# Turned weights of an attention training step: one TensorE pass that stores them, in place of crossbar loads in each stage

## The chip, the cores and the metric

One NeuronCore of a Trainium2 chip runs the whole program. The metric is device time in microseconds (us) of one execution. Three timed runs of the kernel before gave 5001.88, 5009.69 and 5017.44 us; the median is 5009.69 us.

## What is computed

The reference runs a layer and its backward pass. A layer norm gives `xn`. A recurrent attention with 32 heads of 128 walks over 64 segments of 32 tokens; 8 memory rows come out of each segment's output and go into the next. A gated MLP works on the same `xn`.

```python
for s in range(n_seg):                       # 64 segments, one after the other
    h = concat([mem, xn[32*s : 32*s+32]])    # 8 + 32 rows of 640
    q, k, v = h @ Wq, h @ Wk, h @ Wv         # 640 -> 32 heads x 128
    o = softmax(mask(q @ k.T * scale)) @ v @ Wo
    mem = o[:8]; outs.append(o[8:])
s = concat(outs)
g = silu((silu(xn @ w1) * (xn @ w3)) @ w2)
out = x + s * g                              # and the gradients of all nine inputs
```

The forward pass multiplies by Wq, Wk, Wv and Wo. The backward pass multiplies by their transposes. Each of the four weights is 640 x 4096 numbers of bf16, which is 5.24 MB.

## The kernel before

The program is a row of stages; in each stage a call of `in_order` pins the order on every engine to the order in which the code is written.

- **Layer norm and MLP forward** (`phase12_ln_Bfwd`). It also loads Wv and Wk, and ends with projecting the first 672 tokens on Wv.
- **First projections** (`first_part`). The 672 tokens are projected on Wk and then on Wq: 48 steps, each of two banks of five matmuls (L366), a copy of each bank on VectorE and ScalarE, and a 224 KB store on GpSimd's queue (L371). The staging tile `b0st` has three buffers. Six crossbar loads bring the turned tokens `b0x` (L270). Wq and Wo are loaded in nine pieces on ScalarE's queue (L435) in the even steps. The memory rows mem0 are loaded turned, element by element, on GpSimd's queue (L412) at the start of the stage. kT, which the recurrence uses, is cleared by GpSimd memsets (L438). From step 26 on, eight loads `kr` on SyncE's queue (L420) are turned by TensorE (L426).
- **Recurrence** (`recurrence`), 64 dependent segments with the work of all other rows filled into the gaps.
- **Output stage** (`phase3b_out`). 32 units are walked in order: load attention rows `orow` on SyncE's queue (L852), turn them on TensorE (L862), multiply by Wo (L873). From unit 7 on, blocks of `grad_out @ Wo^T` (`gox`, L818) are filled in, which read WoT. The three turned weights WoT, WvT and WkT come in by twelve crossbar loads of 1.31 MB each (`turned_load`, L270), one each in the first four units and then one in every third.
- **Backward recurrence** (`phase4_Abwd`). A prologue of 21 iterations, with 19 units of work for rows, fills in all that the first backward segments need: unit loads on GpSimd's queue (gqv L1169 and L265, gPr L1173), stores of VTD (L1186), DSR (L1217) and GX (L821) on the same queue, stores of GXP (L1233) and loads of gor (L265) on SyncE's queue. Sixteen `gox` blocks ride along; they need the crossbar load `gx` of token rows (SyncE) before block 0 and block 8, and they share one staging tile `gstg`. Four crossbar loads bring WqT, in iterations 1, 4, 7 and 10. Then 64 segments run backward; `packed_half` (L306) reads WoT, `packed_out` (L325) reads WvT, WkT and WqT, all from SBUF.
- **Weight gradients** (`phase6_Awgrads`), eight rounds of four heads. Each round loads three turned weight pieces of 0.66 MB (`ld_w`, L1368) by crossbar into single buffers. In the first round these stand on SyncE's queue between the loads of units 0 to 2 and of units 3 and 4; in the later rounds they are issued before the round's 64 us of `wg` matmuls (L1476).
- **Wo gradient, MLP backward**, which the change doesn't touch.

Of the kernel before, what the change touches and what calls it, by code (L numbers as in the profile page):

```python
# [9 lines left out]
BF16 = mybir.dt.bfloat16  # L10
# [6 lines left out]
P = 128  # L17
# [23 lines left out]
class K:  # L41
# [109 lines left out]
    def setup_dram(self):  # L151
# [45 lines left out]
            self.VTD.append(mk(f"VTD{tl}", (P, ns, H, 40)))  # L197
        self.PM = mk("PM", (T, P, 80))
        self.GSP = mk("GSP", (8, 3, 160, 512))

    def x_src(self, tl, w, c0, c1):
        return self.tok_src(96 * tl, self.geo(tl)[2], w, c0, c1)
# [95 lines left out]
    return ap  # L298


def packed_half(k, bank, x, W, b):

    for dc in range(k.DC):
        for g in range(4):
            c0 = g * 1024 + b * 512
            k.nc.tensor.matmul(bank[32 * g:32 * g + 32, :], x[:, dc, :], W[:, dc, c0:c0 + 512],  # L306
                               start=(dc == 0), stop=(dc == k.DC - 1), tile_position=(0, 32 * g),
                               skip_group_check=True)

# [44 lines left out]
    return pt  # L354


def first_rows(k, ps, stage, xs, off, W, dst, x0, cg, nb=112, tag="b0pb", w=1024, q=None):

    nc = k.nc
    for b in range(2):  # L360
        c0 = cg * 1024 + b * 512
        if w == 512 or b == 0:
            st = stage()
        pb = ps.tile([nb, 512], F32, name="b0pb", tag=tag)
        for dc in range(k.DC):
            nc.tensor.matmul(pb[:], xs[:, dc, x0 - off:x0 - off + nb], W[:, dc, c0:c0 + 512],  # L366
                             start=(dc == 0), stop=(dc == k.DC - 1))
        s0 = b * 512 if w == 1024 else 0
        k.copy(st[:, s0:s0 + 512], pb[:], eng='vs'[b])
        if w == 512 or b == 1:  # L370
            (q or nc.sync).dma_start(dst[x0:x0 + nb, cg * 1024 + (b * 512 if w == 512 else 0):cg * 1024 + b * 512 + 512], st[:])  # L371
# [21 lines left out]
def first_part(k, Wv, Wk_, Wq, Wo, kTs, vt, hxs, rest):  # L393
    nc, tc = k.nc, k.tc
    DC, H, HD = k.DC, k.H, k.HD
    with tc.tile_pool(name="b0", bufs=1) as io, tc.tile_pool(name="b0s", bufs=3) as stp, \
            tc.tile_pool(name="b0p", bufs=4, space=bass.MemoryType.PSUM) as ps, \
            tc.tile_pool(name="b0k", bufs=2, space=bass.MemoryType.PSUM) as pk:
        start = len(nc.cur_bb.bb.instructions)
        xs = io.tile([P, DC, k.NB0], BF16, name="b0x")  # L400
        for x0 in range(0, k.NB0, 112):
# [3 lines left out]
        fetch = [(Wq[:, dc], wq[:, dc]) for dc in range(DC)] + [(Wo[:, h:h + 8], wo[:, h:h + 8]) for h in range(0, H, 8)]  # L405
        for tt in hxs:
            nc.gpsimd.memset(tt[:], 0.0)
        zero = [kTs[0]] + [vt, kTs[1]] + rest
        nc.gpsimd.dma_start(k.m_rows(k.HRO, 0), k.mem0)
        with nc.allow_non_contiguous_dma(reason="tiny mem0 transpose load"):  # L410
            for dc in range(DC):
                nc.gpsimd.dma_start(hxs[0][:, dc, 0:8], k.mem0[:, dc * P:(dc + 1) * P].rearrange("m p -> p m"))  # L412
        rt = io.tile([P, DC, 96], BF16, name="ride0")
        turned_load(k, rt[:], k.XN[k.NB0:k.NB0 + 96, :])
        nc.gpsimd.tensor_copy(hxs[0][:, :, 8:32], rt[:, :, 0:96:4])
# [2 lines left out]
        def kload(i):  # L418
            krs[i] = io.tile([96, 512], BF16, name="kr0", tag="kr0", bufs=2)
            nc.sync.dma_start(krs[i][:], k.KX[0:96, 512 * i:512 * i + 512])  # L420

        def kturn(i):
# [4 lines left out]
            dst = kTs[0][:, i * 4:i * 4 + 4, :].rearrange("p h (s c) -> p h s c", c=40)[:, :, :, 8:40]  # L427
            nc.vector.tensor_copy(dst, pt[:].rearrange("p h (s c) -> p h s c", c=32))

        n = 0  # L430
        for W, dst in ((Wk_, k.KX[:, :]), (Wq, k.QVX[:, 0])):
            for x0 in range(0, k.NB0, 112):
                for cg in range(4):
                    if n % 2 == 0 and fetch:
                        nc.scalar.dma_start(*fetch.pop(0))  # L435
                    first_rows(k, ps, lambda: stp.tile([112, 1024], BF16, name="b0st", tag="b0st"), xs, 0, W, dst, x0, cg, q=nc.gpsimd)
                    if zero:
                        nc.gpsimd.memset(zero.pop(0)[:], 0.0)  # L438
                    if n >= 26 and n % 2 == 0 and (n - 26) // 2 < 9:
                        i = (n - 26) // 2  # L440
                        if i > 0:
                            kturn(i - 1)
                        if i < 8:
                            kload(i)
                    if n == 44:
                        for i in range(2):
                            nc.sync.dma_start(vt[64 * i + 8:64 * i + 40, :], k.QVX[0:32, 1, 2048 * i:2048 * i + 2048])
                    n += 1
# [364 lines left out]
def gx_block(k, xs, sg, pb, WoT, x0, cg, b, eng):  # L813

    w = min(P, k.S - x0)
    c0 = cg * 1024 + b * 512
    for dc in range(k.DC):
        k.nc.tensor.matmul(pb[0:w, :], xs[:, dc, 0:w], WoT[:, dc, c0:c0 + 512], start=(dc == 0), stop=(dc == k.DC - 1))  # L818
    k.copy(sg[0:w, b * 512:(b + 1) * 512], pb[0:w, :], eng='vs'[b])
    if b == 1:  # L820
        eng.dma_start(k.GX0[x0 - k.GB0:x0 - k.GB0 + w, cg * 1024:(cg + 1) * 1024], sg[0:w, :])  # L821


def phase3b_out(k, Wo, W0, W4):
# [2 lines left out]
    nc, tc = k.nc, k.tc  # L827
    D, DC, H, HD, T = k.D, k.DC, k.H, k.HD, k.T
    WT = {}
    WoT = W0.tile([P, DC, HD], BF16, name="WoT", tag="w0")  # L830
    src = k.A_Wo.rearrange("h e d -> (h e) d")
    fetch = [(WoT[:, :, r:r + 1024], src[r:r + 1024, :]) for r in range(0, HD, 1024)]
    for (nm_, src, tag) in (("v", k.A_Wv, "w1"), ("k", k.A_Wk, "w2")):
        WT[nm_] = (W0 if tag == "w1" else W4).tile([P, H, D], BF16, name=f"W{nm_}T", tag=tag)
        src = src.rearrange("d h e -> d (h e)")
        fetch += [(WT[nm_][:, h0:h0 + 8, :], src[:, h0 * P:(h0 + 8) * P]) for h0 in range(0, H, 8)]
    with tc.tile_pool(name="oio", bufs=1) as io, tc.tile_pool(name="oac", bufs=1, space=bass.MemoryType.PSUM) as pa, \
            tc.tile_pool(name="ops", bufs=3, space=bass.MemoryType.PSUM) as ps:
        NRT = k.NO // 4
# [76 lines left out]
        for i, (b, qd) in enumerate(work):  # L916
            if i + 4 < len(work):
                ld(*work[i + 4])
            if fetch and (len(fetch) > 8 or i % 3 == 0):
                turned_load(k, *fetch.pop(0))  # L920
            if i + 1 < len(work):
                turn(*work[i + 1])
            proj(b, qd)
            if late:
                rows_out(*late.pop(0))
            if qd == 7:
                ep_a(b)
                late = [(b, t) for t in range(blocks[b][1])]
            for _ in range(1 if b < 2 else 3):
                if i >= 7 and g0:  # L930
                    gox(*g0.pop(0))
# [8 lines left out]
    n = k.NTL - 1  # L940
# [19 lines left out]
def phase4_Abwd(k, out2, WoT, WvT, WkT, WqT, later):  # L960
# [3 lines left out]
    with tc.tile_pool(name="gst", bufs=1) as st, tc.tile_pool(name="gchain", bufs=1) as ch, \  # L964
# [339 lines left out]
        for i in range(len(pro) + 2):  # L1304
# [2 lines left out]
                    f(*pro[i - o])  # L1307
            if 0 <= i - 2 and (i - 2 + 6 < len(pro) or i >= len(pro) - 2):
                ld_next()
            if i % 3 == 1 and i < 12:  # L1310
                h0 = 8 * (i // 3)
                turned_load(k, WqT[:, h0:h0 + 8, :], k.A_Wq.rearrange("d h e -> d (h e)")[:, h0 * P:(h0 + 8) * P])
            if g0 and i > 0:
                gox(*g0.pop(0))
        assert not g0
# [13 lines left out]
def phase6_Awgrads(k, X, out0, out3, out4, out5):  # L1329
# [12 lines left out]
    with tc.tile_pool(name="h6i", bufs=3) as io, tc.tile_pool(name="h6", bufs=1) as hp, \  # L1342
# [18 lines left out]
            return f"a{base + i % m}"  # L1361

        def ld_w(qd):
            c0 = qd * 512
            ws = []
            for i, src in enumerate((k.A_Wv, k.A_Wk, k.A_Wq)):
                w = gp.tile([P, 4, D], BF16, name="w6", tag=f"w6{i}")
                turned_load(k, w[:], src.rearrange("d h e -> d (h e)")[:, c0:c0 + 512])  # L1368
                ws.append(w)
            Ws[qd] = ws  # L1370

# [723 lines left out]
```

## Time and profile before

| stage | from, us | to, us |
|---|---|---|
| layer norm, MLP forward, first Wv projection | 0 | 282.5 |
| first projections | 282.5 | 412.9 |
| recurrence | 412.9 | 1757 |
| output stage | 1757 | 1882 |
| backward recurrence, prologue | 1882 | 2021 |
| backward recurrence, 64 segments | 2021 | 3132 |
| weight gradients, eight rounds | 3132 | 4420 |
| Wo gradient, MLP backward | 4420 | 4991 |

The profiled execution took 4992.93 us itself; its recorded span is 4991.2 us, so 1.7 us lie around it. It is 16.8 us faster than the median of the three timed runs. Over the span TensorE is busy for 4497.8 us (90%), VectorE for 2211.8 us, ScalarE for 1680.4 us, GpSimd for 1969.0 us; the 16 DMA engines move 836.04 MB, 168 GB/s on average. TensorE's mean granted clock is 0.961.

How to read it: a line of the windows view gives a stretch of time, its length, and then for each engine the time that it was busy and how many instructions it ran, then the granted TensorE clock, the mean busy share of the DMA engines, and the GB/s that they moved. A busy share of DMA can pass 1 in the records. In the view of one source line, "a/b/c" is the shortest, median and longest duration in ns; `SPq` is SyncE's queue, whose durations are times in which the queue issues a transfer, not the transfer itself.

### The profile page before, as it was taken

Reading aid. Unit: us, or ns where it says so; the run is one execution under the profiler, and the core shown is the slowest. Engines: PE = TensorE matmul, PEld = TensorE weight load, DVE = VectorE, ACT = ScalarE, POOL = GpSimd, SP = SyncE. Lnnn points to the kernel's source line nnn. Section 1 sums busy time; section 2 is a strip of 40 time slices with the busy share of each in tenths; the row PEclk is TensorE's granted clock in tenths of the full one; section 3 lists DMA queues with packets and bytes.
Section 4 is the critical chain, followed back from the end, with each engine's and each line's share of the span. In section 5 each row is a group of like instructions: output and inputs, shape, how many; then the busy total and the mean of one; then the engine's idle time right before and its main releaser. Section 6 shows DMA issues by size and latency. Waiting matters only on the chain.

```text
span 4991.2 us, 160105 instructions
## 1 busy us (share of the span) xinstructions
PE 4497.8 (90%) x64274; PEld 2891.4 (58%) x64544; DVE 2211.8 (44%) x7173; ACT 1680.4 (34%) x4768; POOL 1969.0 (39%) x3320
## 2 busy tenths in 40 slices
PE   8888998988898784789999999799999999999999
PEld 4445555555555552556666665556666566667675
DVE  8624555555556522445555554322333233311361
ACT  5422555555555521233333332322233222300000
POOL 6521444444444404345544443533444333411340
PEclk9999999999999886899999999899999999999999
DMA  8653555555555488677777775843565445659783
GB/s 275 219 178 111 164 168 165 168 166 169 165 163 160 127 194 163 175 202 216 214 210 207 205 205 147 179 113 108 130 146 130 107 109 132 164 169 226 163 192 94
DMA packets 1041986, 836.04 MB, mean 168 GB/s; under 512 B 594859, under 2 KB 927391, under 8 KB 1039239
## 3 DMA queue, kind: packets, MB, share of 16 engines
q1 hardware_dynamic: 817639, 547.28, 41.4%
q0 software_dynamic: 127664, 229.32, 16.5%
q10 hardware_dynamic: 95939, 49.18, 3.9%
q8 instruction: 510, 8.36, 0.7%
q14 instruction: 234, 1.91, 0.1%
HBM read 463.32 MB, written 306.24 MB: 154 GB/s over the span
## 4 chain that ended last, share of the span: by engine, by line
PE 48%; DMA 8%; issue 4%; DVE 2%; ACT 2%; SPq 1%; POOL 1%; ACTq 0%; POOLq 0%; DVEq 0%
PE wg L1476 10%; PE gbank L325 8%; PE g L1457 7%; PE oa L1618 3%; DMA dS<-DSR 3%; PE wa L2005 2%; PE pgxb L1938 2%; PE r6p L1408 2%; PE t6g L1439 1%; PE gbank L1086 1%; PE gbank L306 1%; SPq L270 1%; PE pghb L1917 1%; PE sT L873 1%; PE w2a L1861 1%
## 5 line engine op out<-in xcount | busy, mean ns | idle before, releaser
L1476 PE MATMUL wg<-gr,hr 128*128 128x512 bf16 x2352 | 519.1, 379 | 2.5
L1457 PE MATMUL g<-w,ghacc 128*128 128x320 bf16 x3072 | 472.2, 305 | 0.8
L1476 PEld LDWEIGHTS <-hr 128*128 128x128 bf16 x2400 | 233.9, 98 | 278.9
L1457 PEld LDWEIGHTS <-ghacc 128*128 128x128 bf16 x3072 | 294.0, 100 | 110.5 <-ACT ghacc L92 2.2
L713 POOL DMA_DIRECT2D OR<-xv x163 | 93.1, 571 | 452.2 <-ACT xv L712 337.2
L306 PEld LDWEIGHTS <-hx 128*32 128x32 bf16 x7680 | 177.2, 96 | 162.5 <-issue 1.0
L90 DVE CAST wgo<-wg 128x512 bf16<-128x512 f32 x72 | 49.8, 692 | 471.2 <-PE wg L1476 462.9
L90 DVE CAST stg<-bank 128x512 bf16<-128x512 f32 x256 | 177.1, 692 | 179.8 <-PE bank L306 176.0
L92 ACT COPY ghacc<-t6g 128x768 bf16<-128x768 bf16 (+1 forms) x176 | 137.2, 780 | 350.9 <-PE t6g L1439 348.1
L664 ACT ACTIVATE xP<-xsp,xnm 120x120 bf16<-120x120 f32 (+1 forms) x704 | 240.6, 376 | 9.3 <-DVE xnm L660 5.6
L325 PEld LDWEIGHTS <-gkv 128*8 128x8 bf16 x8192 | 178.8, 87 | 83.5 <-issue 3.4
L1186 POOL DMA_DIRECT2D VTD<-gvT x176 | 129.2, 740 | 237.5 <-ACT gvT L1185 209.4
L1423 POOL DMA_DIRECT2D GSP<-grs x48 | 25.7, 547 | 476.9 <-ACT grs L1415 475.2
L675 POOL TENSOR_TENSOR xP<-xP,xrz 120x480 bf16<-120x480 bf16 x163 | 161.7, 992 | 125.2 <-ACT xP L664 88.7
L1463 DVE TENSOR_TENSOR ghacc<-ghacc,g 128x320 f32<-128x320 f32 x192 | 93.6, 487 | 223.3 <-PE g L1457 223.3
L92 ACT CAST wgo<-wg 128x512 bf16<-128x512 f32 x48 | 28.1, 586 | 479.8 <-PE wg L1476 421.4
L1215 DVE SCALAR_TENSOR_TENSOR gdS<-gdp,Dx,gPr 120x120 bf16<-120x120 f32 (+1 forms) x680 | 183.0, 332 | 0.0
L306 PE MATMUL gbank<-WoT,gox 128*32 128x512 bf16 x2560 | 154.1, 388 | 19.6 <-POOL gox L1005 13.5
L325 PE MATMUL bank<-Wo,oTm 128*32 128x320 bf16 x4032 | 171.5, 322 | 0.1
L539 DVE COPY vt<-stg 8x512 bf16<-8x512 bf16 x512 | 160.9, 314 | 21.8 <-ACT stg L92 13.9
L325 PE MATMUL gbank<-WvT,gkv 128*8 128x320 bf16 x4096 | 169.5, 309 | 0.0
L1233 POOL DMA_DIRECT2D GXP<-gks x157 | 91.5, 583 | 192.9 <-ACT gks L1231 190.3
(343 smaller groups left out, 10817.2 us busy)
## 6 DMA issues: line engine op xcount, KB each, us to landing
QVS<-stg SPq DMA_DIRECT2D x128, 256.0 KB
vTt<-VTD SPq DMA_DIRECT2D x64, 320.0 KB
VTD<-gvT POOLq DMA_DIRECT2D x168, 120.0 KB, 4.0
DSR<-gdS POOLq DMA_DIRECT2D x168, 120.0 KB, 3.2
dS<-DSR SPq DMA_DIRECT2D x168, 120.0 KB
P<-PR SPq DMA_DIRECT2D x168, 120.0 KB
PR<-xP POOLq DMA_DIRECT2D x163, 120.0 KB, 3.2
OR<-xv POOLq DMA_DIRECT2D x163, 120.0 KB, 2.6
```

Of the source, the lines that this page charges most:

```text
L90: return nc.vector.tensor_copy(out, in_)
L92: return nc.scalar.copy(out, in_)
L306: k.nc.tensor.matmul(bank[32 * g:32 * g + 32, :], x[:, dc, :], W[:, dc, c0:c0 + 512], start=(dc == 0), stop=(dc == k.DC - 1), tile_positio ...
L325: k.nc.tensor.matmul(pm[p0:p0 + nq, 0:320], x[:, h, :], W[:, h, 320 * b:320 * b + 320], start=(first and i == 0), stop=(last and i == 15), ...
L539: nc.vector.tensor_copy(vt[p0:p0 + 8, c0:c0 + 512], sv[32 * g:32 * g + 8, b * 512:(b + 1) * 512])
L664: nc.scalar.activation(Pb[0:n, j, 0:n], sp[0:n, j, :], ACT.Exp, bias=nmx[0:n, j:j + 1], scale=k.scale, accum_out=Z[0:n, j:j + 1])
L675: eng.tensor_tensor(Pb[0:n, :, 0:n], Pb[0:n, :, 0:n], bc_last(rz[0:n], n), ALU.mult)
L1186: nc.gpsimd.dma_start(k.VTD[tl][:, :, h0:h0 + 4, :], vTq[:])
L1215: nc.vector.scalar_tensor_tensor(dS[0:n, j, 0:n], dp[0:n, j, :], Dx[0:n, j:j + 1], Pr[0:n, j, 0:n], op0=ALU.subtract, op1=ALU.mult)
L1457: nc.tensor.matmul(pg[:], ring[:, i, j, r0:r0 + P], Ws[qd][i][:, j, 320 * h:320 * h + 320], start=(i == 0 and j == 0), stop=(i == 2 and j ...
L1476: nc.tensor.matmul(pw[:], hr[:, tl, dc * P:(dc + 1) * P], grs[i][:, tl, :], start=(tl == 0), stop=(tl == NF - 1))
L1618: nc.tensor.matmul(ac[j][i][:], orr[:, w, jj * P:(jj + 1) * P], gow[:, w, 320 * i:320 * i + 320], start=(w == 0), stop=(w == NW - 1))
```

## The change

A DRAM tensor `WTD` takes the four turned weights. The first projections make them: a helper `turn_w` takes one head of one weight, does five TensorE transposes of 128 x 128 into a new PSUM tile `wpt0` (two buffers), copies the 128 x 640 result on ScalarE or VectorE in turn into one of six slots of a ring that lies in the second kT tile, and stores the slot (160 KB) on SyncE's queue. There are 4 x 32 = 128 such heads. Eight are done ahead of the first step; each step then does two between its matmuls and, in two of three steps, one more, so that the last comes in step 44. Around this the stage is rearranged: `b0st` gets a fourth buffer, the loads of Wq and Wo move to the odd steps, the loads of mem0 move to step 20, and the memset of the second kT tile moves to step 46.

The later stages load `WTD` by ordinary DMAs, 0.66 MB each, on the same queue as before: 24 in the output stage (two per unit in the first four units, then one per unit), eight in the prologue of the backward recurrence (iterations 1 to 8), three per round in the weight gradients. WoT's layout in SBUF changes from `[128, 5, 4096]` to `[128, 32, 5, 128]`, so the 512 columns that a matmul reads are four runs of 128 (`wcols`).

```diff
+        self.WTD = mk("WTD", (4, P, H, D))
...
+def wcols(W, dc, c0):
+    return W[:, c0 // P:c0 // P + 4, dc, :] if len(W.shape) == 4 else W[:, dc, c0:c0 + 512]
...
         for dc in range(k.DC):
             nc.tensor.matmul(pb[:], xs[:, dc, x0 - off:x0 - off + nb], W[:, dc, c0:c0 + 512],
                              start=(dc == 0), stop=(dc == k.DC - 1))
+        if mid:
+            mid()
...
-    with tc.tile_pool(name="b0", bufs=1) as io, tc.tile_pool(name="b0s", bufs=3) as stp, \
+    with tc.tile_pool(name="b0", bufs=1) as io, tc.tile_pool(name="b0s", bufs=4) as stp, \
...
-        zero = [kTs[0]] + [vt, kTs[1]] + rest
-        nc.gpsimd.dma_start(k.m_rows(k.HRO, 0), k.mem0)
...
+        zero = [kTs[0], vt] + rest
+
+        def mem_ld():
+            nc.gpsimd.dma_start(k.m_rows(k.HRO, 0), k.mem0)
+            with nc.allow_non_contiguous_dma(reason="tiny mem0 transpose load"):
+                for dc in range(DC):
+                    nc.gpsimd.dma_start(hxs[0][:, dc, 0:8], k.mem0[:, dc * P:(dc + 1) * P].rearrange("m p -> p m"))
+        turns = [(i, h) for i in (0, 1, 3, 2) for h in range(H)]
+        ring = kTs[1][:].rearrange("p h c -> p (h c)").rearrange("p (r c) -> p r c", c=k.D)
+        tn = [0]
+        def turn_w():
+            if not turns:
+                return
+            i, h = turns.pop(0)
+            pt = pw.tile([P, DC, P], BF16, name="wpt0", tag="wpt0")
             for dc in range(DC):
+                src = Wo[:, h, dc * P:(dc + 1) * P] if i == 3 else (Wv, Wk_, Wq)[i][:, dc, h * P:(h + 1) * P]
+                nc.tensor.transpose(pt[:, dc, :], src, k.ident[:])
+            sl = ring[:, tn[0] % 6, :]
+            k.copy(sl.rearrange("p (a b) -> p a b", b=P), pt[:], eng='sv'[tn[0] % 2])
+            tn[0] += 1
+            nc.sync.dma_start(k.WTD[i, :, h, :], sl)
...
+        for _ in range(8):
+            turn_w()
...
-                    if n % 2 == 0 and fetch:
+                    if n % 2 == 1 and fetch:
                         nc.scalar.dma_start(*fetch.pop(0))
-                    first_rows(k, ps, lambda: stp.tile([112, 1024], BF16, name="b0st", tag="b0st"), xs, 0, W, dst, x0, cg, q=nc.gpsimd)
+                    first_rows(k, ps, lambda: stp.tile([112, 1024], BF16, name="b0st", tag="b0st"), xs, 0, W, dst, x0, cg, q=nc.gpsimd, mid=turn_w)
+                    if n % 3 != 2:
+                        turn_w()
...
+                    if n == 20:
+                        mem_ld()
+                    if n == 46:
+                        nc.gpsimd.memset(kTs[1][:], 0.0)
...
-    WoT = W0.tile([P, DC, HD], BF16, name="WoT", tag="w0")
-    src = k.A_Wo.rearrange("h e d -> (h e) d")
-    fetch = [(WoT[:, :, r:r + 1024], src[r:r + 1024, :]) for r in range(0, HD, 1024)]
...
+    WoT = W0.tile([P, H, DC, P], BF16, name="WoT", tag="w0")
+    src = k.WTD[3].rearrange("p h (dc e) -> p h dc e", e=P)
+    fetch = [(WoT[:, h0:h0 + 4], src[:, h0:h0 + 4]) for h0 in range(0, H, 4)]
...
+        fetch += [(WT[nm_][:, h0:h0 + 4, :], k.WTD[i, :, h0:h0 + 4, :]) for h0 in range(0, H, 4)]
...
-            if fetch and (len(fetch) > 8 or i % 3 == 0):
-                turned_load(k, *fetch.pop(0))
+            for _ in range(2 if len(fetch) > 16 else 1):
+                if fetch:
+                    nc.sync.dma_start(*fetch.pop(0))
...
-            if i % 3 == 1 and i < 12:
-                h0 = 8 * (i // 3)
-                turned_load(k, WqT[:, h0:h0 + 8, :], k.A_Wq.rearrange("d h e -> d (h e)")[:, h0 * P:(h0 + 8) * P])
+            if 1 <= i < 9:
+                h0 = 4 * i - 4
+                nc.sync.dma_start(WqT[:, h0:h0 + 4, :], k.WTD[2, :, h0:h0 + 4, :])
...
-                turned_load(k, w[:], src.rearrange("d h e -> d (h e)")[:, c0:c0 + 512])
+                nc.sync.dma_start(w[:], k.WTD[i, :, 4 * qd:4 * qd + 4, :])
```

## The prediction

> **What bounds the kernel now.** I read the stage table first, then the windows view of the stages that the change touches, since the average over the span hides them.
>
> ```profile
> 284.00:294.00 10.00, 0.00 (x0) 0.00 (x0) 0.00 (x0) 0.00 (x0) 3.93 (x5) 0.53 0.58 140
> 294.00:340.00 46.00, 39.81 (x165) 22.93 (x166) 10.25 (x15) 8.79 (x15) 21.12 (x27) 0.92 0.76 254
> 360.00:410.00 50.00, 50.00 (x258) 30.43 (x257) 18.25 (x31) 13.28 (x23) 12.07 (x23) 1.00 0.38 121
> 1755.00:1800.00 45.00, 30.25 (x272) 23.36 (x272) 6.96 (x20) 5.69 (x12) 0.00 (x0) 0.77 1.01 217
> 1900.00:2021.00 121.00, 50.44 (x504) 30.54 (x512) 34.15 (x224) 25.42 (x97) 49.70 (x85) 0.61 0.78 166
> ```
>
> In the first projections TensorE waits for tokens at 284 to 294 us, loses 6 us by 340 us while Wq and Wo come in, and is then the bound: 50 of 50 us, DMA only 0.38 busy. Its work there can't be hidden. The output stage is the opposite: the DMA engines are full (1.01) and TensorE idles 15 of 45 us. In the prologue of the backward recurrence TensorE works 50 of 121 us. The view of the crossbar line shows how long each load holds SyncE's queue:
>
> ```profile
> L270 SPq DMA_TRANSPOSE w<-in_A_Wv_dram x8: 2413/2548/3618, 3142.4 to 4199.5; - x8
> ...
> L270 SPq DMA_TRANSPOSE WoT<-in_A_Wo_dram x4: 5122/6258/8044, 1762.7 to 1784.5; - x4
> L270 SPq DMA_TRANSPOSE WvT<-in_A_Wv_dram x4: 5608/6577/7377, 1792.2 to 1827.6; - x4
> L270 SPq DMA_TRANSPOSE WkT<-in_A_Wk_dram x4: 5882/6636/7507, 1840.0 to 1875.3; - x4
> L270 SPq DMA_TRANSPOSE WqT<-in_A_Wq_dram x4: 5367/6336/9972, 1894.0 to 1965.0; - x4
> ```
>
> The chain of waits in the prologue (start, length, what) has four long pieces, each beside one WqT load (1894.0, 1915.5, 1934.3, 1965.0 us on SyncE's queue):
>
> ```profile
> 1894.02 5.37 SPq L270
> 1899.43 4.87 DMA gx<-GS
> ...
> 1920.63 11.00 DMA gqv<-QVS
> ...
> 1936.02 15.19 DMA VTD<-gvT
> ...
> 1966.23 10.32 DMA gqv<-QVM
> ```
>
> **What the Trainium skill says.** "DMA: Bandwidth & Descriptors", Latency and other measured facts, gives 261 GB/s for crossbar transposes of this kind. The trace agrees: the output stage's first 38 us move 249 GB/s with the engines full; an ordinary mix reached 375 to 393 GB/s at 330 to 342 us. The same page, Queues, rings and completion order, says that each DMA engine goes round its rings packet by packet, so a bulk load slows every other queue: GX stores land in 12.5 us (median) at 1910 to 1940 us, where two WqT loads run, and in 4.0 at 1940 to 1965, by the view of DMA issues. "TensorE: Matmul & The Clock Gate", Part 4, puts a transpose at about 275 ns in a kernel and says its result must be copied out of PSUM. The trace differs on the rate: four of 96 x 96 (L426) hold TensorE for 0.17 us (370.35 to 370.52), 43 ns each; I use the trace.
>
> **First projections: the cost.** One head is five transposes; scaled from 96 to 128 columns, 57 ns each, 0.28 us. Eight heads run before the tokens land and cost nothing if that wait stays; it does, since the tokens' loads are first on SyncE's queue. 120 heads x 0.28 = +34 us on TensorE's path. The copies, 64 x 0.69 us on ScalarE (same shape, L1687: 694 ns) and 64 x about 0.48 us on VectorE (from 354 ns at 384 columns and 400 ns at 480), lie beside TensorE: per step of 2.9 us ScalarE then has 1.5 us, VectorE 1.4. They would cost about 75 us if they were serial. SyncE's 128 issues (0.4 us each) and the `kr` loads behind them fit too.
>
> At the start, SyncE issues seven crossbar loads (9.1 us) ahead of the first store. The mem0 and Wq loads no longer stand before them, so I put the first at 286.5 instead of 290.4 (it waits for QVX stores; 2.8 us landing). The first stored slot is then free at about 299; the ring of six is full and head 8 waits for it, so step 0 ends at about 301 us instead of 296.7.
>
> Then the DMA engines may bind. Steps 1 to 17 carry 10.5 MB of Wq and Wo, 17 x 2.67 x 0.164 = 7.4 MB of turned heads and 17 x 0.229 = 3.9 MB of projections: 21.8 MB. At 350 GB/s (between the 301 and 393 of 330 to 348 us) that is 62 us, where TensorE needs 17 x 2.91 = 49.5. Steps 18 to 47 need 30 x 2.16 + 27 x 0.75 + 1.4 = 86.5 us, at 229 GB/s. The stage ends at 301 + 62 + 86.5 = 449.5 against 412.9: **+36 us**, with +24 if DMA never binds and +58 in the third case below. The mem0 loads at step 20 take GpSimd 4.5 us and land in 6.9; four staging buffers (11.6 us) cover them, and without that cover they cost about 5. The memset at step 46 delays one store by 3.3 us, and no one waits for it.
>
> **Output stage.** Twelve loads with 5 to 8 us on SyncE's queue become 24 with about 0.4 us. Bytes are the same: 15.7 MB, 45 us at 350 GB/s instead of 63 at 249. From unit 1 at 1770.1 us the unhindered step is 2.96 us, so unit 7's turn would start at 1784.9, not 1794.5: 9.6 us, plus 2.3 us of cold clock after the two stalls. Later idle time, 5 us after 1800, gives 1 or 2. **-13 us** (-5 to -17: six units load 0.95 MB in 3 us, so `orow` may be late again, by up to 8 us).
>
> **Prologue.** WqT's issues fall from 28 us of SyncE's queue to 3. Without the load ahead, `gx` starts 5 us sooner. The three stalls behind the others (8.8 and 8.5 us of TensorE waiting for `gdS` at 1923 and 1938, and up to 10.9 near 1966) and the late second `gx` (12.5 us, 5 of which stay) shrink. What is late next is the single `gstg` tile: pairs of blocks come every 6.6 us with small units and 8.5 to 9.2 with large ones, as at 1978 to 1996. So 1899.5 + 4 x 6.6 + 5 + 4 x 9 + 11.7 (last units) + 13 (loads before the first segment) = 1991.6, and 4 to 5 us for 5.2 MB of plain WqT in the first eight iterations: 1996 against 2021, **-25 us** (-10 to -38).
>
> **Weight gradients.** In round 0 three loads hold the queue from 3142.4 to 3152.4; TensorE waits 10.9 us for `dS` until 3156.6. Plain, 1.97 MB ahead on the ring take about 5 us, so `dS` lands near 3151: **-5 us** (-2 to -8). In the seven other rounds nothing: 64 us of `wg` matmuls with DMA 0.24 busy hide the loads either way.
>
> **WoT's layout.** Four runs of 128 columns for 2560 + 72 + 154 matmuls. `gdp` reads runs of 32 (L1200): 120 columns in 70 ns in two instructions, no slower than plain ones. I take 0; 10% of the 2.34 us of 40 matmuls would be 64 x 0.23 = 15 us. A gain is excluded: the same columns are read.
>
> **Sum.** 36 - 13 - 25 - 5 = -7 us: 4993 becomes 4986 in the profiled execution. The median of the runs lies 16.8 us above that execution, so I forecast 5003 us.
>
> **Rivals.** (1) As above, 50%, own range 4983 to 5023. (2) DMA keeps up and the prologue runs at `gstg`'s pace: 24 - 14 - 36 - 6 = -32, 4978; for it speak 393 GB/s at 330 us, against it KX stores that stall TensorE already with less traffic. 25%. (3) Slower: the ring of six. A head can be copied only when the store of six heads ago has landed. With a landing of L plus 0.4 us issue and 0.7 us copy, a step of 2.67 heads takes 2.67/6 x (L + 1.1); this decides over TensorE's 2.91 us from L = 5.4 us on. KX stores landed in up to 6.6 us in this stage. L = 7.7 would be 3.9 us per step over 45 steps: 24 + 44 = +68, net +25: 5035. 17%. (4) The strided read costs 10%: net +8, 5018, 8%.
>
> **Chances.** About 0.3% (15 us) is what a measurement of this kernel tells from no change. Faster: 0.12 of case 1 and 0.23 of case 2. Slower: 0.15 of case 3, 0.03 of case 4, 0.02 of case 1. The rest is the same. The range 4970 to 5036 leaves out the far ends of cases 2 and 3.
>
> **What would show it.** The recurrence's first matmul near 450 us (437 for case 2, 470 or more for case 3); no idle time on TensorE over 2 us in steps 18 to 44; no TensorE wait above 2 us between 1766 and 1800's counterpart; a prologue of about 114 us, and GX landing near 4 us; L306 on gbank still 2.34 us per 40. Wrong it would be if stores to WTD land in over 6 us, or if the prologue keeps its 10 us waits.

## The result

The changed kernel takes as long as the one before. The first measurement gave a median of 5008.73 us against 5006.85, ratio 1.0004 (95% interval 0.9983 to 1.0025). A longer one, 19 executions against 25, gave 5006.43 us against 5010.81, ratio 0.9993 (0.9983 to 1.0003). By this ratio the change is worth -3.5 us, with an interval of -8.5 to +1.5 that takes in zero.

The profiled execution of the changed kernel took 5009.31 us, its span is 5007.6 us. The windows view of it, with the stretches that answer to those of before (start of the first projections, their first half, a stretch of the second half, the start of the output stage, the prologue):

```profile
284.00:294.00 10.00, 6.35 (x51) 3.90 (x50) 2.17 (x4) 2.66 (x4) 0.41 (x2) 0.87 0.39 90
294.00:391.00 97.00, 76.11 (x557) 50.18 (x557) 31.49 (x57) 35.71 (x57) 27.29 (x40) 0.91 0.86 280
405.00:455.00 50.00, 50.00 (x420) 34.47 (x418) 24.34 (x47) 24.58 (x39) 9.01 (x17) 1.00 0.73 239
1817.00:1862.00 45.00, 34.56 (x335) 26.66 (x336) 9.26 (x26) 7.62 (x16) 0.00 (x0) 0.85 0.94 260
1953.00:2048.00 95.00, 53.30 (x516) 30.73 (x518) 34.07 (x224) 25.65 (x97) 49.37 (x84) 0.63 0.72 211
```

The ten idle microseconds at 284 now hold the 40 transposes of the first eight heads; the other 11 matmuls of that line are the end of the Wv projection and the first bank of step 0. The first 24 steps last to 391 us, and TensorE is idle for 21 of these 97 us, more than before; the second half runs at TensorE's pace with DMA at 0.73 where it was 0.38. In the output stage TensorE is busy for 34.6 of 45 us instead of 30.3. The prologue does the same work (516 matmuls after 504) in 95 us instead of 121.

The view of the source lines that load `WTD` shows what SyncE's queue was freed of: 320 to 450 ns in the median for an issue, where a crossbar load of twice the size held it for 5 to 10 us (in the weight gradients, with the same size as now, 2.4 to 3.6 us).

```profile
L956 SPq DMA_DIRECT2D WoT<-WTD x8: 320/448/493, 1824.0 to 1834.7; - x8
L956 SPq DMA_DIRECT2D WvT<-WTD x8: 319/322/465, 1839.6 to 1869.6; - x8
L956 SPq DMA_DIRECT2D WkT<-WTD x8: 320/449/951, 1871.5 to 1906.8; - x8
...
L1348 SPq DMA_DIRECT2D WqT<-WTD x8: 414/426/460, 1943.8 to 1982.8; - x8
...
L1403 SPq DMA_DIRECT2D w<-WTD x24: 319/332/1380, 3162.3 to 4207.3; - x24
```

In the prologue's chain of waits (start, length, what) the pieces of 10 to 15 us behind gqv and VTD are gone. The long pieces left are the two loads of `gx` and the stores of the one `gstg` tile:

```profile
1943.81 0.42 SPq L1348
1944.27 8.24 DMA gx<-GS
...
1967.70 7.96 DMA GX<-gstg
...
1980.23 6.24 DMA GX<-gstg
...
1989.91 4.29 DMA gx<-GS
```

### The profile page after: what moved, and what is told of

Its sections match the earlier page's. It is cut to its first block, busy times and chain, and to the rows that moved or that the text cites. A ratio compares the mean times of both kernels' runs of the same rounds, so it can differ in the third digit from the quotient of the medians.

```text
span 5007.6 us, 162091 instructions
## 1 busy us (share of the span) xinstructions
PE 4588.8 (92%) x65184; PEld 2925.8 (58%) x65184; DVE 2240.8 (45%) x7237; ACT 1721.3 (34%) x4832; POOL 1969.3 (39%) x3320
## 4 chain that ended last, share of the span: by engine, by line
PE 42%; issue 9%; DMA 7%; POOL 2%; DVE 2%; ACT 2%; SPq 1%; POOLq 0%; ACTq 0%; DVEq 0%
PE gbank L331 9%; PE wg L1511 6%; PE g L1492 5%; PE oa L1653 3%; DMA dS<-DSR 2%; PE wa L2040 2%; PE pgxb L1973 1%; PE r6p L1443 1%; PE gbank L1122 1%; PE t6g L1474 1%; POOL r L244 1%; PE gbank L312 1%; DMA r<-QVS 1%; DMA ggtok<-ggT 1%; PE pghb L1952 1%
## 5 line engine op out<-in xcount | busy, mean ns | idle before, releaser
L1458 POOL DMA_DIRECT2D GSP<-grs x48 | 25.7, 548 | 477.3 <-ACT grs L1450 476.4
L244 POOL DMA_DIRECT2D r<-GOS x256 | 144.7, 569 | 61.1 <-issue 20.0
```

The costliest lines, as they stand in the source:

```text
L244: eng.dma_start(d, src if src.shape[0] > 1 else src[0])
```

## The stages in nine profiles

One profile of each kernel can't tell 10 us from chance, so here are the stages of all kernels that were run with crossbar loads in the stages that the change doesn't touch. Times are us, measured on TensorE: the first projections run from the last matmul of the Wv projection to the first one of the recurrence, the recurrence to its own last four matmuls, the output stage from there to its own last one, the prologue to the first matmul of the 64 segments. The labels are those of the experiments below; "before" and "after" are the first profiles.

| kernel | first projections | recurrence | output stage | prologue | weight gradients |
|---|---|---|---|---|---|
| before | 130.8 | 1342.8 | 125.5 | 139.8 | 1285.9 |
| before_again | 128.5 | 1347.9 | 125.9 | 142.2 | 1292.4 |
| after | 174.9 | 1357.4 | 117.2 | 113.6 | 1275.0 |
| after_again | 168.5 | 1351.8 | 125.1 | 112.8 | 1275.1 |
| make_only | 170.4 | 1358.4 | 126.2 | 136.0 | 1285.0 |
| no_store | 154.6 | 1355.1 | 126.5 | 139.7 | 1284.4 |
| load_only | 130.9 | 1346.6 | 117.1 | 111.4 | 1285.9 |
| paced | 174.7 | 1355.8 | 121.6 | 111.6 | 1272.2 |
| wq_only | 141.1 | 1347.0 | 127.2 | 113.9 | 1284.1 |

Three more kernels with no crossbar load at all and two variants of them follow further down. The 64 backward segments lie between 1101 and 1110 us and the MLP backward between 392 and 402 in this table's kernels, with no order in it.

My first theory (A): a trade, in which the making costs some 44 us, the plain loads give back about as much, and the 15 us that the unchanged recurrence took longer are chance. The rival (B): the change makes the recurrence slower by itself.

## Experiments

**The changed kernel again** (`after_again`), nothing edited.

> The changed kernel, unaltered, timed and profiled once more. Theory A (a trade): the first projections cost about 44 us more, the output stage, the prologue of the attention's backward pass and the weight gradients give back 8.6, 26.2 and 10.8 us, and the 14.8 us that the recurrence took longer in the profiled execution (1366.0 against 1351.2 us, with not one instruction of it changed) are a difference between executions. Then the ratio is 0.998 to 1.002 and this profile's recurrence lies anywhere from 1350 to 1366 us, while the four stages that the change touches stay within 2 us of the first profile's. Theory B: the change itself makes the recurrence slower by about 15 us (what it leaves behind in memory or in the clock), and that has eaten a gain. Then the recurrence is 1364 to 1368 us here too.

Measured: ratio 0.9993 (0.9983 to 1.0003). Prologue and weight gradients came within 1 us of the first profile; the first projections are 6 us shorter and the output stage 8 us longer, so these two vary more than I said. The recurrence is 1360.2 us as the expectation counts it, up to the first turn of the output stage (1351.8 in the table, which stops 8 us earlier): in A's range, and below the 1364 to 1368 of B.

**The kernel before again** (`before_again`), nothing edited.

> The kernel before, unaltered, profiled once more, because its first profile shows an execution at 4992.9 us where the median of its runs is about 5010: which stages hold the 18 us? Theory A (the spread lies in stages that the change doesn't touch, the recurrence above all): at about 5010 us its recurrence takes 1352 to 1358 us (first profile: 1343 by the first matmul of the output stage), its first projections 131 us, its prologue 137 to 140, its weight gradients 1285 to 1287 us. Theory B (the changed kernel's recurrence is slower by itself): the recurrence of before stays at 1343 to 1347 us.

Measured: 5006.82 us, recurrence 1347.9 us. Theory A had 1352 or more, B up to 1347. Of the 14 us that this execution is longer than the first profile, 5 lie in the recurrence, 6.5 in the weight gradients, 4 in the MLP backward. That began to speak for B.

**The making alone** (`make_only`). The later stages got their crossbar loads back:

```diff
-            for i in range(3):
-                w = gp.tile([P, 4, D], BF16, name="w6", tag=f"w6{i}")
-                nc.sync.dma_start(w[:], k.WTD[i, :, 4 * qd:4 * qd + 4, :])
+            for i, src in enumerate((k.A_Wv, k.A_Wk, k.A_Wq)):
+                w = gp.tile([P, 4, D], BF16, name="w6", tag=f"w6{i}")
+                turned_load(k, w[:], src.rearrange("d h e -> d (h e)")[:, c0:c0 + 512])
...
```

> The changed first projections alone: the weights are turned and stored there, and nobody reads them; the output stage, the prologue and the weight gradients load by the crossbar as before. Theory A: the making costs 44 to 47 us, so about 5053 us, ratio 1.009; the later stages take what they took before (118, 139 and 1289 us). Theory B: the recurrence is slower as well, 59 to 62 us in all, ratio 1.012.

Measured: 5038.41 us, ratio 1.0051 (1.0035 to 1.0067), +25.5 us by the ratio: less than both theories. Its stages say more, +40 in the first projections and +13 in the recurrence against the mean of the two profiles of before. The kernel before had its longest median, 5010.81 us, in this group; in three later groups it was 4994.2 to 4997.9. Within the group the making and the loads add up: 5038.4 + 4964.3 (next run) - 5006.4 = 4996.3 is what the kernel before would take if the two parts made the whole, and it lies among the medians of the later groups. I take the differences between kernels of one group as better founded than the one to the kernel before.

**The loads alone** (`load_only`). The first projections of before; the loads of the change, from the weights as given, in the same sizes:

```diff
-                nc.sync.dma_start(w[:], k.WTD[i, :, 4 * qd:4 * qd + 4, :])
+                nc.sync.dma_start(w[:], flatw(k, i)[:, 4 * qd:4 * qd + 4, :])
```

> The changed loads alone: the first projections are those of before, nothing is turned or stored, and the later stages load plainly, by descriptors of the same size and number, from the weights as they lie in memory, unturned (so the numbers of those stages are computed from the wrong weights). Theory A: minus 46 us, about 4961 us, ratio 0.991, in the places 118 to 109, 139 to 113 and 1289 to 1278 us, and a recurrence like that of before. Theory B: minus 46 or somewhat more too; here the two don't part. A rival of the reading that the loads earn the 46: part of it is a difference between executions, and the ratio is 0.994 or above.

Measured: 4964.32 us, ratio 0.9926 (0.9897 to 0.9955), near the 0.991 of theory A, and 42 us below the changed kernel of the same group. The output stage and the prologue are as fast as in the changed kernel. The weight gradients are not: 1285.9 us, no gain. More on that below.

**Making without stores** (`no_store`): `make_only` with one line fewer.

```diff
-            nc.sync.dma_start(k.WTD[i, :, h, :], sl)
```

> The changed first projections with the turning and its copies out of PSUM, but without the 128 stores of 160 KB; later stages load by the crossbar as before (so it computes all that the reference wants, and the turned weights are dropped). It parts TensorE's share of the making from that of the stores and of the ring of six buffers that waits for them. If the stores cost what lies above TensorE's own time: first projections 160 to 167 us (131 plus 128 heads at 0.28 us less the idle time that they fill), against 168.5 to 174.9 with stores. If the ring and the stores cost nothing: 168 to 175 us again. Of the recurrence theory B of the first runs, if it is the stores, expects 1343 to 1347 us here, and if it is the turning, 1352 to 1358.

Measured: 5024.24 us, ratio 1.0055 (1.0034 to 1.0075); first projections 154.6 us, less than either reading had, and 16 us less than `make_only`, which has the stores. TensorE stands for 10.1 us in this stage (its gaps over 0.25 us), for 20.9 and 18.7 in the two profiles of the kernel before, for 24.3 and 19.9 in the two of the changed kernel. So the turns themselves are (154.6 - 10.1) - (130.8 - 20.9) = 34.6 us of TensorE for 128 heads, 0.27 us each; they fill about 10 us of the old idle time, and the stores bring as much or more new idle time in. The windows view of `no_store` (first half and second half of the stage) beside that of the changed kernel above:

```profile
284.00:391.00 107.00, 96.94 (x779) 65.83 (x778) 43.25 (x79) 49.27 (x78) 31.31 (x50) 0.98 0.60 179
391.00:438.00 47.00, 47.00 (x376) 31.94 (x375) 21.89 (x43) 21.62 (x35) 8.75 (x17) 1.00 0.30 96
```

The second half is TensorE's own time with or without stores. The first half isn't. The view of waits of the changed kernel in this stage (sum, times, longest) names who waits: the copies into the ring, for stores of six heads ago.

```profile
ACT kT L92 <- DMA WTD<-kT: 37.7, 12, 9.9
DVE kT L90 <- DMA WTD<-kT: 32.1, 10, 10.3
```

By the DMA packets of the trace a store lands 1.4 us after its issue at best, 2.5 in the median, and mostly 4 to 8.3 between 305 and 376 us, while Wq and Wo come in. The recurrence of `no_store`, 1355.1 us, also took the stores off the list for theory B.

**The fetches spread** (`paced`): Wo's 5.2 MB are fetched after step 24, and Wo is turned last.

```diff
-        turns = [(i, h) for i in (0, 1, 3, 2) for h in range(H)]
+        turns = [(i, h) for i in (0, 1, 2, 3) for h in range(H)]
...
-                    if n % 2 == 1 and fetch:
+                    if n in (1, 5, 9, 13, 17, 25, 27, 29, 31):
```

> The changed kernel with its DMA spread over the first projections: Wq is fetched at every fourth step instead of every second, Wo only from step 25 on, and Wo is turned last; the ring of six, the number of turns and their places are the same. Moves 5 MB out of the first 24 steps. If the DMA engines' throughput made the first 24 steps take 99 us (0.9 to 1.0 of their time at 295 to 355 GB/s): these steps come to 83 to 88 us, the stage to 157 to 163 us, the kernel to minus 10 us or so against the changed kernel, ratio 0.997 to before. If the ring's length made it (each store's landing of some us, whatever the load): stage unchanged at 168 to 175 us, ratio 0.9985 to 1.0003.

Measured: ratio 0.9998 (0.9985 to 1.0012), stage 174.7 us. By the stage alone the ring's reading won. The steps say otherwise (times from ScalarE's copies, one a step):

| kernel | steps 1 to 17 | steps 18 to 23 | steps 24 to 47 |
|---|---|---|---|
| before | 46.3 | 14.7 | 53.2 |
| after | 67.3 | 20.1 | 69.2 |
| after_again | 63.4 | 17.7 | 69.2 |
| no_store | 57.9 | 18.2 | 69.2 |
| paced | 53.3 | 21.9 | 81.4 |
| wq_only | 48.5 | 14.8 | 60.6 |

The loss went where the bytes went: 10 to 14 us off steps 1 to 17, 12 us onto steps 24 to 47, where Wo's four fetches now stand in seven steps. The windows view of `paced` shows it in TensorE's busy time, 88.9 of 107 us and then 61.8 of 67:

```profile
284.00:391.00 107.00, 88.86 (x686) 59.43 (x685) 36.56 (x66) 42.88 (x68) 29.82 (x46) 0.95 0.79 251
391.00:458.00 67.00, 61.83 (x466) 41.58 (x466) 28.37 (x54) 27.62 (x44) 10.89 (x21) 0.92 0.79 264
```

So the loss follows the load on the DMA engines; that it reaches TensorE through the short ring is what the waits above show, but no kernel with a longer ring was run. "DMA: Bandwidth & Descriptors", Queues, rings and completion order, of the Trainium skill says that each DMA engine takes turns between the queues that have work for it, a packet at a time; that a bulk load then slows the other queues was the prediction's own step from there. The stores beside the large fetches, mostly 4 to 8.3 us where the median of all is 2.5, agree with that.

**Only Wq turned** (`wq_only`): one head a step from step 12 on; Wo, Wv and Wk by crossbar as before.

```diff
+        turns = [(2, h) for h in range(H)]
...
+                    if n >= 12:
+                        turn_w()
...
+            if 1 <= i < 9:
+                h0 = 4 * i - 4
+                nc.sync.dma_start(WqT[:, h0:h0 + 4, :], k.WTD[0, :, h0:h0 + 4, :])
...
+                if i == 2:
+                    nc.sync.dma_start(w[:], k.WTD[0, :, 4 * qd:4 * qd + 4, :])
```

> Only Wq is turned by TensorE, one head a step from step 12 on, where the DMA queues are half idle; its turned copy serves the prologue and Wq's part of the weight gradients; Wo, Wv and Wk go by the crossbar as before. Theory A: 32 heads at 0.28 us add 9 us to the first projections, with no wait of theirs; the prologue gives 26 us and the weight gradients 0 to 4: minus 17 to minus 21, about 4988 us, ratio 0.996. Rival: the prologue's gain needs the faster output stage ahead of it (the transposes of that stage still lie in SyncE's queue), and comes out at half: minus 4 to minus 8 us, ratio 0.999.

Measured: 4982.25 us, ratio 0.9945 (0.9925 to 0.9966), 24 us below the changed kernel of the same group: the one kernel here that leaves nothing out and beats both. (The kernel before had its longest median in this group; the stages in the table give -18 against its two profiles.) By stages: +11 us in the first projections and -27 in the prologue. The prologue's gain doesn't need the faster output stage ahead of it. In the windows view (the first 13 steps or so, then step 21 or so to the end) TensorE waits as before (gaps over 0.25 us in the stage sum up to 19.7 us, 20.9 and 18.7 before), and of the later 66 us 1.1 are idle:

```profile
294.00:340.00 46.00, 37.95 (x168) 22.20 (x169) 9.98 (x15) 8.69 (x15) 17.31 (x25) 0.87 0.75 232
360.00:426.00 66.00, 64.90 (x411) 41.09 (x409) 27.14 (x47) 21.74 (x37) 14.24 (x27) 1.00 0.53 167
```

**The recurrence.** By now four profiles without the turning of all four weights had 1342.8 to 1347.9 us and five with it 1351.8 to 1358.4, with no overlap. Theory A was wrong there. The order of instructions in the recurrence and what each waits for are the same in both programs, so I compared GpSimd's queue step by step. Here is GpSimd's timeline at the same store (the 84th of 163), first in the changed kernel, then in `wq_only` (start, length, what; idle before it in brackets):

```profile
1174.60 0.98 POOL L711 TENSOR_TENSOR xP<-xP,xrz 120x480 bf16<-120x480 bf16 x1 [1.91 <-ACT xP L700]
1178.81 0.59 POOL L712 DMA_DIRECT2D PR<-xP  x1 [3.23 <-DVE hx L633]
1179.42 1.00 POOL L711 TENSOR_TENSOR xP<-xP,xrz 120x480 bf16<-120x480 bf16 x1
```

```profile
1141.65 0.98 POOL L697 TENSOR_TENSOR xP<-xP,xrz 120x480 bf16<-120x480 bf16 x1 [1.90 <-ACT xP L686]
1142.93 0.60 POOL L698 DMA_DIRECT2D PR<-xP  x1 [0.30 <-POOL xP L697]
1143.54 1.00 POOL L697 TENSOR_TENSOR xP<-xP,xrz 120x480 bf16<-120x480 bf16 x1
```

The store of `PR` is issued 3.23 us after the multiplication instead of 0.30, and TensorE, which turns the next `xP`, stands for 2.4 us. This comes four times in every profile of a kernel that turns all four weights, at the same four of the 163 stores, and never in the others. The kernel before has such stalls too, one DMA issue earlier. Where two stores of `OR` follow each other, GpSimd's gaps ahead of them are 5.77 and 0.07 us before, 2.84 and 2.67 us after; the pattern comes four times in the recurrence, and nobody waits there. One issue ahead of the late `PR` stands a store of `PM`, after which GpSimd waits for ScalarE anyway (1.9 us in the lines above); whether a stall of the kernel before is hidden there, the trace doesn't show. The view of waits in the recurrence shows it on TensorE, before and after:

```profile
PE xpp L683 <- POOL xP L675: 4.4, 3, 2.2
```

```profile
PE xpp L719 <- POOL xP L711: 10.2, 7, 2.4
```

TensorE's gaps ahead of all turns of `xP`, whoever ends them, come to 11.3 to 12.0 us in the four profiles and to 17.1 to 19.5 in the other five: between six and seven of the +9 us. Where the rest lies is open.

**No crossbar load anywhere.** The last five kernels load the same bytes plainly wherever the changed kernel turns by crossbar. The base (`plain_base`):

```diff
-    k.nc.sync.dma_start_transpose(dst, src)
+    k.nc.sync.dma_start(dst, src.rearrange("r c -> (r c)").rearrange("(p a w) -> p a w", p=dst.shape[0], a=dst.shape[1]))
...
```

> The changed kernel with every crossbar load replaced by a plain load of the same bytes, not turned (all stages that read turned data compute from wrong numbers; what is left out is the turning by the DMA). It is the base for the next two. The first projections keep TensorE's 128 turns, the ring of six buffers, the 128 stores and the nine large fetches, and lose only the crossbar loads ahead of them, so their first stores are not held up behind SyncE: TensorE's first wait of 7 us there should shrink, and the stage take 160 to 168 us against 168.5 to 174.9. If the later waits of the stage are due to crossbar loads and not to the fetches: below 158 us.

Measured: 4965.52 us, ratio 0.9943 (0.9921 to 0.9965), first projections 160.6 us with TensorE idle for 14.7 (gaps over 0.25 us); the first wait shrank from 6.4 to 3.9 us. Three variants with the same first projections, but for a few memsets in two of them (below), had 170.0 to 175.9 us, so 160.6 isn't typical: this stage differs by up to 15 us between executions. Nearly all of that lies in the first 24 steps. In steps 1 to 17 the same 20 MB moved at 341 GB/s in `plain_base` (59.3 us), at 285 and 286 in `plain_flat` and `shift3` (70.4 us each) and at 311 in `shift20` (64.6 us), while steps 24 to 47 take 69.2 us in all four. Why the rate differs is open.

**Small fetches** (`plain_fine`).

```diff
-        fetch = [(Wq[:, dc], wq[:, dc]) for dc in range(DC)] + [(Wo[:, h:h + 8], wo[:, h:h + 8]) for h in range(0, H, 8)]
+        fetch = [(Wq[:, dc, c:c + 1024], wq[:, dc, c:c + 1024]) for c in range(0, HD, 1024) for dc in range(DC)] + \
+            [(Wo[:, h:h + 2], wo[:, h:h + 2]) for h in range(0, H, 2)]
...
-                    if n % 2 == 1 and fetch:
+                    if fetch:
```

> Like the one with every crossbar load replaced by a plain one (wrong numbers in the same stages), and the same bytes of Wq and Wo fetched in smaller pieces: 20 of 256 KB and 16 of 320 KB, one a step, instead of nine of 1.0 and 1.28 MB at every second step; Wo is turned last. In the changed kernel a store lands 1.4 to 2.5 us after its issue where no fetch runs and 4 to 8 us after it beside one. If these bursts make the ring of six too short: stores land within about 3 us and the stage is 8 to 14 us shorter than its base's, the kernel by as much. If it is the ring whatever the load, or the mean load: within 3 us of its base.

Measured: 4956.66 us, ratio 0.9929 (0.9907 to 0.9950), which overlaps the base's; first projections 159.5 us. Steps 1 to 17 take 51.7 us (59.3 to 70.4 in the four kernels with large fetches), steps 24 to 47 take 76.1 instead of 69.2, since Wo comes there. Nine tenths of the stores land within 4.4 us, 5.5 in the base. It points the way of `paced`: fewer bytes in the first steps help them and load the later ones. Whether small pieces help beyond that is not settled.

**Where the weight gradients read** (`plain_flat`).

```diff
-                nc.sync.dma_start(w[:], k.WTD[i, :, 4 * qd:4 * qd + 4, :])
+                nc.sync.dma_start(w[:], (k.A_Wv, k.A_Wk, k.A_Wq)[i].rearrange("d h e -> (d h e)").rearrange("(p h d) -> p h d", p=P, d=D)[:, 4 * qd:4 * qd + 4, :])
```

> Like the one with every crossbar load replaced by a plain one (wrong numbers in the same stages), and the weight gradients' 24 loads taken from the weights as given, with the same sizes and strides, instead of from the stored turned copies. With the loads changed alone the weight gradients took 1285.9 us, with the whole change 1272.2 to 1275.1. If the place that is read matters: 8 to 13 us longer than its base in the weight gradients. If that profile was an odd one, or another part of the change brought the 11 us: within 3 us of its base.

Measured: 4965.29 us, ratio 0.9945 (0.9924 to 0.9965); weight gradients 1275.6 us, 1279.2 in the base, 1282.4 in `plain_fine`. So there is no sign that the place that is read matters. The 1285.9 us of `load_only` lie above the other plain profiles, which span 1272 to 1282 us; I found no cause for them. Crossbar profiles span 1284 to 1292 (`wq_only`, with a third of its loads plain, 1284.1). The changed kernel with crossbar loads in this stage alone was not measured.

**GpSimd's stalls** (`shift3` and `shift20`): a few more instructions on GpSimd ahead of the first projections of `plain_base`.

```diff
+        for _ in range(3):
+            nc.gpsimd.memset(hxs[1][:, 0, :], 0.0)
```

> Like the one with every crossbar load replaced by a plain one (wrong numbers in the same stages), with three more tiny memsets of GpSimd ahead of the first projections, at about 0.1 us each. In all eight profiles of kernels that turn all four weights, GpSimd issues the store of the softmax PR four times in the recurrence 3.5 to 4.2 us after the multiplication of its operand, where it takes 1.28 us everywhere else, at its records 666, 1032, 1397 and 2127, 365 or 366 apart; in the four profiles without, never, with the same instructions and waits in the recurrence; the recurrence takes 1351.8 to 1358.4 us against 1342.8 to 1347.9. If these are stalls of GpSimd at fixed distances in its own stream, which the change has moved by one record onto a place where TensorE waits: three records more move them off it, the four late stores are gone or elsewhere, and the recurrence is 1342 to 1349 us. If they come from the turning, the stores or the start time: still four, and 1352 to 1358 us.

> The same with twenty more memsets of GpSimd, some 2 us in all ahead of the first projections. If stalls sit at fixed distances in GpSimd's stream, they come 20 records earlier in the program of the recurrence, where its stores of the attention's output and its copies are: four late stores of PR are gone, and the recurrence is 1342 to 1349 us, unless one of the new places is on TensorE's path too. If the stalls belong to the turning or the start time: as before, 1352 to 1358 us.

Measured: 4971.44 us, ratio 0.9945 (0.9928 to 0.9963), and 4965.96 us, ratio 0.9936 (0.9916 to 0.9957); recurrence 1358.0 and 1350.9 us. The four late stores are there in both, at the same four stores, though GpSimd has run 3 and 20 instructions more by then. My reading, stalls at fixed distances in GpSimd's instructions, fell. What stays: they go by GpSimd's DMA issues. Before the four late stores it has issued 243, 364, 485 and 727; at 606, the one that is missing in steps of 121, a store of `PM` is 2.7 us late. The change moves six DMAs of that queue, the loads of mem0, from ahead of the first projections to step 20; the four profiles without the stalls have them at the start, `wq_only` too. So the moved loads of mem0 are the suspect, but I didn't move them alone, and the cause stays open. The turning of all four weights, as the rival in these two runs, isn't excluded, nor are the fourth `b0st` buffer and the moved fetches, which `wq_only` doesn't have either; the stores (`no_store`), the crossbar (`plain_base`) and the moved memset of the second kT tile (`wq_only` has it) are.

## Why the prediction was right, and where it wasn't

The forecast, 5003 us and most likely no change clear of noise, came true, but in part by luck. The sum was -7 us. The same terms as measured on the stages, with one that the sum left out, come to +8: five errors of 2 to 9 us, not all of one sign, which add up to 15 us and happen to stay within what can't be told from no change. The profiled execution, for which the prediction had 4986 us, took 5009.31.

**First projections, +36: right in its working, a little short.** I put the end of step 0 at 301 us, steps 1 to 17 at 62, steps 18 to 47 at 86.5. The two profiles have 303.0 and 300.0, 67.3 and 63.4, 89.3 and 86.9. The stage costs 168.5 to 174.9 against 128.5 to 130.8 us, +42 by the means. The term that was too small is the DMA-bound one: by the DMA packets, steps 1 to 17 moved 20.2 MB (21.8 were priced) at 300 and 318 GB/s, not 350. TensorE's 34 us, for 120 heads, is close to what `no_store` gave for 128 (34.6). After the first eight heads and one bank of step 0 TensorE stood for 6.4 us until the first store had landed and the ring had a free slot, as I had said. Loads of mem0 cost no wait of TensorE there; they may cost the recurrence something, see below.

**Output stage, -13: the right kind, too large.** The two profiles gave -8.5 and -0.6 (other kernels with plain loads -4 to -9), about -6. The step that failed is that `orow` would be in time: TensorE waited for it again, 1.7 us once in the first profile, 2.6 and 2.9 us in the second, where it had been 3.0 and 3.2 before. The rate behind it was too high as well: the first 45 us moved 260 GB/s with the engines 0.94 busy, not 350. I had named the late `orow` at the low end of the range.

**Prologue, -25: right**, -27 over four profiles with crossbar loads and five without. WqT's share of that is all of it (`wq_only` 113.9 us). What came sooner is above all the unit loads `gqv`, which go by GpSimd's queue and not by SyncE's. In the view of DMA issues (number, KB each, median us from issue to landing), before at 1900 to 2021 us and after at 1953 to 2048:

```profile
gqv<-QVS POOLq DMA_DIRECT2D x7, 192.0 KB, 10.8
```

```profile
gqv<-QVS POOLq DMA_DIRECT2D x7, 192.0 KB, 5.1
```

In `before_again` it is 10.2 us, in `after_again` 3.9, in `wq_only` 4.7. The reasons given were partly off. The GX stores, whose 4.0 us in the prediction is a single store, took 7.2 and 5.0 us in the median over the whole prologue in the two profiles of before and 5.2 and 4.6 in those of after, so little came from them. Waits for `gdS` shrank from 8.8, 8.5 and 10.9 us to 5.4, 4.8 and 4.8 without going. The `gx` wait at the second block fell from 12.6 to 5.6, as said.

**Weight gradients, -5, of round 0 only: mis-sized.** Means are 1286.9 us with crossbar loads (four profiles) and 1277.1 with plain ones (four), -10, but with 1285.9 among the latter. The wait for `dS` that I priced went from 10.9 and 11.1 us to 9.1 and 9.8, so it gave 1 to 2 us; the rest is spread over the rounds: TensorE's gaps over 0.3 us sum up to 65 and 70 us in the two profiles of before and to 61 and 59 in those after. "In the seven other rounds nothing" was wrong, if the difference is the loads' at all: the 1285.9 us of `load_only`, with plain loads, lie in the range of the crossbar.

**WoT's layout, 0: right.** The 2560 matmuls of `gbank` take 379 ns in the median in both kernels.

**What the sum had no term for: the recurrence, +9.** I took a stage whose code doesn't change as unchanged. Six to seven of the nine are TensorE's waits beside GpSimd's late stores. The prediction priced the mem0 loads with 5 us at most where they now stand, but not what moving DMAs does to the rest of GpSimd's queue, if it was that.

The measured terms make +42 - 6 - 27 - 10 + 9 = +8 us; the timed runs say -3.5 (-8.5 to +1.5). Most of the difference of 11 us lies in which executions were profiled: the two of before took 4992.93 and 5006.82 us, by their mean 10.9 below the median of 5010.81 that the timed comparison has, the two of after 5009.31 and 5003.92, at their median of 5006.43. So the stages account for the profiled executions, which differ by +7, and whether the change gains or loses a few us, these runs don't tell: the median of the kernel before itself moves between 4994 and 5011 us from group to group.

Of the rivals, (2), DMA keeping up, fell with steps 1 to 17 at 63 to 67 us. (3), the ring deciding over all 45 steps, fell with the second half at TensorE's pace, 2.88 us a step, stores landing in 1.4 to 3.5 us there; in the first half the landing did pass its 5.4 us, and some stores took over 6, which the prediction had named as a sign of being wrong. There the ring does hold TensorE up. (4) fell with the 379 ns.

## What to carry to other kernels

A stage bound by TensorE pays for every transpose that is put into it (0.27 us for a head of 640 x 128), so turn there only what a later stage is really late for: one weight in four brought 27 of the 43 us of gain, for 11 of the 42 us of cost, and left the recurrence as it was. Bytes that are added to a stage with the DMA engines 0.38 busy are only free if they don't meet the stage's own fetches; count each stretch of steps by itself and look at where a moved fetch goes. And compare stages that a change doesn't touch over several profiles before calling a difference chance: here it was 9 us, and it was real.

## What the runs showed that I had not expected

- GpSimd's queue stands for 2.2 to 2.9 us, with nothing in the profile to wait for, at places in the recurrence that lie 121 of its DMA issues apart (after 243, 364, 485, 606 and 727 of them in the kernels that turn all four weights), whatever else it computes (3 or 20 more instructions moved nothing); where such a stall falls decides whether it costs up to 2.4 us of TensorE or nothing.
- The profile names the engine whose event came last as the releaser of such a stall (VectorE's `hx`, 0.4 us earlier), though the store doesn't wait for it. The same place in another kernel's profile told that.
- First projections that are the same but for a few memsets took 160.6, 170.0, 171.4 and 175.9 us in four kernels, with TensorE idle for 14.7 to 25.7 us of it.
